# Loading gates, keys and queries four tokens to a packet, with the gate weights issued by ScalarE and the first products on a tile of ones

## The chip, the core and the metric

The kernel runs on one core of a Trainium2 chip. The core has five engines that work side by side and wait for each other by semaphores: TensorE (PE in the profile, with PEld for its weight loads), VectorE (DVE), ScalarE (ACT), GpSimd (POOL) and SyncE (SP, which only issues DMAs here). Sixteen DMA engines move data between the main memory and the core's own memory of 128 partitions. The metric is the device time of one execution in microseconds (us).

## The reference

A gated linear attention over 4 batches, 8 heads, 768 tokens and 48 columns a head, and behind it a mixture of 8 experts that takes each token's 384 columns:

```python
f = 1.0 / (1.0 + np.exp(-f_logit))
for t in range(S):
    state = f[:, :, t, :, None] * state + np.einsum('bhd,bhe->bhde', k[:, :, t], v[:, :, t])
    y[:, :, t] = np.einsum('bhd,bhde->bhe', q[:, :, t], state)
x = y.transpose(0, 2, 1, 3).reshape(B * S, H * D)
logits = x @ w_gate
expert_idx = np.argmax(logits, axis=1)
# each expert takes its first `capacity` tokens, in order
h = np.maximum(np.einsum('ecd,edf->ecf', disp, w1), 0.0)
y = np.einsum('ecf,efd->ecd', h, w2)
# out[i] = gate_w[i] * (the row of y that token i took), 0 for a token that found no place
```

## The kernel before

The tokens are worked on in 24 chunks of 128 (six to a batch). Instead of one token after the other, a chunk uses products of gates: DVE scans the transposed gates once backwards (`Suf`, line 386) and once forwards (`Rq`, line 400), the keys are multiplied by the one and the queries by the other (line 415), and PE then makes the scores of the whole chunk (`psA`, line 426), masks and all, the product with the values (`psY`, line 522), and an update of the state (lines 488 and 508).

The layout of the loads matters here. For gates (`ld_f`), keys and queries (`ld_kq`) a partition holds two tokens that follow each other, for all eight heads: a piece of 2 x 48 numbers is contiguous in the main memory, 384 bytes. A chunk thus takes 64 partitions; gates of two chunks, or the keys and the queries of one, fill the 128. Values (`ld_v`) have one token to a partition, in pieces of 192 bytes. Before the transposes the pieces are written apart into padded tiles: gates by ACT with the sigmoid (`sig`, line 357, into `pf`), keys and queries by a copy (`kq_pad`, line 407 on POOL and later line 409 on ACT, into `kqp`). `transposes` (line 366) then turns 64 partitions at a time, one pair of heads and one of the two tokens in each call, into `psF` (gates) or `psT` (keys and queries) with every second column written.

Chunk by chunk the work runs in slots: slot n has the values of chunk n, the scores of n + 1, keys and queries of n + 2 (`kq_in`) and gates of n + 3 (`f_in`, `decay`). The order in each engine's queue is that in which the code writes it; every engine works through its queue in order. `prologue` writes the work ahead of slot 0: products that have no use but to occupy PE (`keep_busy`, line 376, on the identity matrix that POOL builds), the gates, keys and queries of the first chunks, and the constants that come late (`late_constants`, line 282: four small DMAs that put the gate weights of the experts into `identc`). All loads but one half of the first gates are issued by SP, in one queue. The queue also stops at a load whose buffer is still read. Loads take turns on eight semaphores, so an issue also waits until the one eight places earlier on the same semaphore has landed.

Attention ends at about 144 us; the experts' products follow.

## Time and profile before

| | |
|---|---|
| time, median of 3 runs | 375.02 us (374.31 to 376.33) |
| the profiled execution | 375.17 us |
| its span, first to last instruction | 373.4 us |
| PE busy | 362.1 us, 97% |
| DVE busy | 247.8 us, 66% |
| ACT busy | 223.8 us, 60% |
| POOL busy | 166.5 us, 45% |
| mean granted clock of PE | 0.990 |

Busy time of PE is modelled and pipelined, so 97% does not say that PE works at its peak. The granted clock is a share of 2.4 GHz, so 0.50 is 1.2 GHz. The chain of waits goes back from the last instruction to what released it, step by step. In the timeline, merged instructions stand in one row, and the brackets say how long the engine was idle before it and what ended that.

### The profile page before, as it was taken

Reading aid. Unit: us, or ns where it says so; the run is one execution under the profiler, and the core shown is the slowest. Engines: PE = TensorE matmul, PEld = TensorE weight load, DVE = VectorE, ACT = ScalarE, POOL = GpSimd, SP = SyncE. Lnnn points to the kernel's source line nnn. Section 1 sums busy time; section 2 is a strip of 40 time slices with the busy share of each in tenths; the row PEclk is TensorE's granted clock in tenths of the full one; section 3 lists DMA queues with packets and bytes.
Section 4 is the critical chain, followed back from the end, with each engine's and each line's share of the span. In section 5 each row is a group of like instructions: output and inputs, shape, how many; then the busy total and the mean of one; then the engine's idle time right before and its main releaser. Section 6 shows DMA issues by size and latency. Waiting matters only on the chain.

```text
span 373.4 us, 10082 instructions
## 1 busy us (share of the span) xinstructions
PE 362.1 (97%) x3895; PEld 340.8 (91%) x3895; DVE 247.8 (66%) x533; ACT 223.8 (60%) x458; POOL 166.5 (45%) x275
## 2 busy tenths in 40 slices
PE   8999999999899999999999999999999999999993
PEld 7999898888787889999899999999999999999993
DVE  4898988979687866753676296857757665570300
ACT  3356677877586763255477475759578586583310
POOL 6665556675757675235613702127117244144012
PEclk9999999999899999999999999999999999999997
DMA  8999999999997432476696979799797997721001
GB/s 153 187 177 224 205 207 227 256 214 226 213 227 164 130 114 105 133 237 204 191 239 188 286 196 242 212 187 319 169 204 247 172 208 253 129 94 52 14 23 40
DMA packets 111351, 67.86 MB, mean 182 GB/s; under 512 B 93646, under 2 KB 105844, under 8 KB 111296
## 3 DMA queue, kind: packets, MB, share of 16 engines
q1 hardware_dynamic: 107504, 57.09, 69.1%
q0 software_dynamic: 3520, 9.97, 7.7%
q8 instruction: 32, 0.52, 0.6%
q14 instruction: 23, 0.19, 0.2%
q10 hardware_dynamic: 272, 0.10, 0.1%
HBM read 49.46 MB, written 11.43 MB: 163 GB/s over the span
## 4 chain that ended last, share of the span: by engine, by line
PE 84%; issue 8%; ACT 3%; POOL 2%; DVE 1%; POOLq 1%; ACTq 0%
PE psM L1222 15%; PE psA L754 9%; PE psM L1015 9%; PE psT L754 9%; PE psM L754 7%; PE psA L426 6%; PE psY L522 6%; PE psA L543 5%; PE psT L366 4%; PE psY L468 3%; PE psA L488 3%; PE psT L451 3%; PE psF L366 2%; POOL out_dram L326 2%; PE psA L376 2%
## 5 line engine op out<-in xcount | busy, mean ns | idle before, releaser
L326 POOL DMA_INDIRECT out_dram<-yo,g_ti x30 | 31.3, 1042 | 55.6 <-ACT yo L1019 31.7
L434 POOL TENSOR_SCALAR_AFFINE_SELECT AT<-AT 128x512 f32<-128x512 f32 x48 | 29.4, 637 | 23.3 <-ACT AT L432 23.2
L1015 PE MATMUL psM<-w2h,hh 128*128 128x384 f32 (+2 forms) x112 | 37.5, 340 | 0.0
L1015 PE MATMUL psM<-w2l,hh 128*128 128x384 f32 (+2 forms) x112 | 37.3, 338 | 0.0
L1015 PE MATMUL psM<-w2h,hl 128*128 128x384 f32 (+2 forms) x112 | 37.2, 338 | 0.0
L135 ACT ACTIVATE w2h<-raw 128x768 fp32r<-128x768 f32 x32 | 27.0, 844 | 11.2 <-DMA raw<-in_moe_w_dram 11.2
L1222 PE MATMUL psM<-hh,w2h 128*128 128x440 f32 (+3 forms) x96 | 33.7, 351 | 0.0
L1222 PE MATMUL psM<-hh,w2l 128*128 128x440 f32 (+3 forms) x96 | 33.7, 351 | 0.0
L1222 PE MATMUL psM<-hl,w2h 128*128 128x440 f32 (+3 forms) x96 | 33.6, 350 | 0.0
L144 DVE TENSOR_TENSOR w2l<-raw,w2h 128x768 fp32r<-128x768 f32 x28 | 27.8, 994 | 7.7 <-ACT w2h L135 6.9
L386 DVE TENSOR_TENSOR_SCAN Suf<-psF,direv 112x511 f32<-112x511 f32 x24 | 29.1, 1212 | 4.5 <-PE psF L366 4.5
L432 ACT ACTIVATE AT<-psA 128x512 f32<-128x512 f32 x48 | 26.4, 612 | 8.9 <-PE psA L426 5.6
L1242 POOL COPY yo<-yq 128x384 uint16<-128x384 uint16 (+4 forms) x16 | 11.9, 790 | 40.1 <-DMA yq<-yp 38.2
L426 PE MATMUL psA<-qT,kT 48*128 48x128 f32 x384 | 29.4, 293 | 0.0
L400 DVE TENSOR_TENSOR_SCAN Rq<-psF,d 112x512 f32<-112x512 f32 x24 | 29.4, 1223 | 0.0
L326 POOL DMA_INDIRECT disp<-rows,ri x24 | 24.8, 1034 | 9.5 <-issue 4.3
L144 DVE TENSOR_TENSOR w1l<-raw,w1h 128x1024 fp32r<-128x1024 f32 x21 | 26.5, 1269 | 2.9 <-ACT w1h L135 2.6
L761 DVE SCALAR_TENSOR_TENSOR hl<-psA,hh 128x224 fp32r<-128x224 f32 (+8 forms) x26 | 14.2, 547 | 21.3 <-ACT hh L760 19.3
L559 ACT ACTIVATE rows<-psA 128x384 f32<-128x384 f32 x24 | 11.8, 491 | 26.0 <-PE psA L543 19.6
L522 PE MATMUL psY<-AT,ld_v 128*48 128x128 f32 (+1 forms) x384 | 26.9, 278 | 0.0
L426 PEld LDWEIGHTS psA<-qT,kT 48*128 48x128 f32 x384 | 25.8, 201 | 0.5 <-issue 0.5
L135 ACT ACTIVATE w1h<-raw 128x1024 fp32r<-128x1024 f32 x24 | 24.8, 1060 | 1.9 <-DMA raw<-in_moe_w_dram 1.9
(253 smaller groups left out, 1041.7 us busy)
## 6 DMA issues: line engine op xcount, KB each, us to landing
raw<-in_moe_w_dram SPq DMA_DIRECT2D x24, 512.0 KB
raw<-in_moe_w_dram SPq DMA_DIRECT2D x32, 384.0 KB
ld_kq<-in_k_dram SPq DMA_DIRECT2D x24, 192.0 KB
ld_kq<-in_q_dram SPq DMA_DIRECT2D x24, 192.0 KB
ld_v<-in_v_dram SPq DMA_DIRECT2D x24, 192.0 KB
ld_f<-in_f_logit_dram SPq DMA_DIRECT2D x11, 384.0 KB
xg<-disp SPq DMA_DIRECT2D x6, 589.5 KB
xg<-disp SPq DMA_DIRECT2D x3, 393.0 KB
```

Source lines behind the costliest of these rows:

```text
L135: return nc.scalar.activation(hi, raw, AF.Copy)
L144: engine.tensor_tensor(lo[cs], raw[cs], hi[cs].bitcast(F32), op=ALU.subtract)
L326: ins = nc.gpsimd.indirect_dma_start(out=dst, out_offset=bass.IndirectOffsetOnAxis(ap=idx, axis=0), in_=rows, in_offset=None, bounds_check ...
L386: nc.vector.tensor_tensor_scan(out=_view(Suf[:R], m - 1, [[-1, m]]), data0=_view(F, m, [[-1, m]]), data1=_view(direv[:R], m - 1, [[-1, m]] ...
L400: nc.vector.tensor_tensor_scan(out=Rq[:R], data0=F, data1=d1[:R], initial=0.0, op0=ALU.mult, op1=ALU.max)
L426: nc.tensor.matmul(pas[s][:, p], kTs[n][r, p], qTs[n][r, p], start=True, stop=True)
L432: nc.scalar.activation(AT[:, s], pas[s], AF.Copy)
L434: nc.gpsimd.affine_select(AT[:, s], AT[:, s], pattern=[[0, NP], [1, C]], compare_op=ALU.is_ge, fill=0.0, base=0, channel_multiplier=-1)
L522: nc.tensor.matmul(py[b][64 * g : 64 * g + m, a, :], vt[:, 2 * p + s, :m], AT[:, s, p, :], start=(first(n) and a == 0), stop=(a == NP // 2 ...
L754: nc.tensor.matmul(ph[:, :T], a[:, c, fs], x[:, c, :T], start=(n == 0), stop=(n == 3 * DT - 1))
L1015: nc.tensor.matmul(py[:n], x[:, ks], a[:, ft], start=(ft == 0 and m == 0), stop=(ft == FT - 1 and m == 2))
L1222: nc.tensor.matmul(pys[c][:, :T], a[:, ft, cs], x[:, :T], start=(ft == 0 and n == 0), stop=(ft == FT - 1 and n == 2))
```

## The change

Gates, keys and queries now have four tokens to a partition, in pieces of 4 x 48 numbers (768 bytes). Each partition holds four heads only, so a chunk takes two times 32 partitions: heads 0 to 3 on the first 32, heads 4 to 7 on the next. `load_quads` takes the place of `pairs` and issues a DMA for each half, so that a load of keys, or of queries, is two DMAs, and one of gates for two chunks is four. `transposes` has four tokens and two pairs of heads in its loops instead of two and four; the number of calls is the same, each writes every fourth column of two pairs.

At the start a tile of ones (`hot`, the first 128 columns of the ring of rows, which is now made earlier) is written by DVE, and `keep_busy` multiplies it by itself, eight times first instead of seven. The gates' transposes of chunk 0 get a second stream beside them, on the other 64 partitions, that transposes the ones into a PSUM tile that nobody reads. The sigmoid of chunk 0 is cut in two along the heads. The four DMAs of `late_constants` move from SP to ScalarE's queue, behind the sigmoids of chunk 0. The pad of chunk 0 is cut in keys and queries, and their transposes are made one after the other instead of in turn. The loads of the third keys and queries, of the first values and of the third gates are written later in the code.

```diff
+    ring = abuf.tile([P, RING, W], F32, name="rows", bufs=1)
+    hot = ring[:, 0, :P]
+    nc.vector.memset(hot, 1.0)
...
-                t = apool.tile([P, H, 2, D], F32, name=f"ld_{nm}{i}")
+                t = apool.tile([P, NP, 4, D], F32, name=f"ld_{nm}{i}")
...
-    def pairs(nm, n, nt):
+    def load_quads(t, r, nm, n, queues):
         b, t0 = n // CPB, n % CPB * C
-        return srcs[nm][b, :, t0 : t0 + nt, :].rearrange("h (t j) d -> t h (j d)", j=2)
+        for i, queue in enumerate(queues):
+            queue.dma_start(
+                t[r + 32 * i : r + 32 * i + 32].rearrange("t h j d -> t h (j d)"),
+                srcs[nm][b, NP * i : NP * i + NP, t0 : t0 + C, :].rearrange("h (t j) d -> t h (j d)", j=4),
+            )
...
         if nm == "kq":
             for h, x in enumerate(nm):
-                nc.sync.dma_start(t[64 * h : 64 * h + 64], pairs(x, n, C))
+                load_quads(t, 64 * h, x, n, (nc.sync, nc.sync))
         elif n == 0:
...
+            load_quads(t, 0, nm, 0, (nc.sync, nc.scalar))
         else:
-            nc.sync.dma_start(t, pairs(nm, 2 * n, 2 * C))
+            for h in range(2):
+                load_quads(t, 64 * h, nm, 2 * n + h, (nc.sync, nc.sync))
...
-                nc.sync.dma_start(identc[64 * g : 64 * g + D, b::2, 2 * D :], gates_of[b, g ^ b])
+                nc.scalar.dma_start(identc[64 * g : 64 * g + D, b::2, 2 * D :], gates_of[b, g ^ b])
...
-        cuts = (0, 64, P) if u == 0 else (0, P)
+        cuts = ((0, 64, 0, 2), (0, 64, 2, NP), (64, P, 0, NP)) if u == 0 else ((0, P, 0, NP),)
...
+            if (r1, h1) == (64, NP):
+                late_constants()
...
-        for p in range(NP):
-            for j in range(2):
+        for p in range(2):
+            for j in range(4):
                 for t, src, h in dsts:
                     r = slice(64 * h, 64 * h + 64)
                     nc.tensor.transpose(
-                        t[:R, p, j::2], src[r, j, 2 * p : 2 * p + 2].rearrange("t s d -> t (s d)")[:, :R], ident[r, r]
+                        t[:R, p::2, j::4], src[r, j, 2 * p : 2 * p + 2].rearrange("t s d -> t (s d)")[:, :R], ident[r, r]
                     )
+                if beside is not None:
+                    nc.tensor.transpose(beside[:R, p::2, j::4], hot[64:, :R], ident[64:, 64:])
...
-            nc.tensor.matmul(pw, ident, ident, start=True, stop=True)
+            nc.tensor.matmul(pw, hot, hot, start=True, stop=True)
...
+        beside = None if ns[0] else psA.tile([P, NP, C], F32, name="psA")
...
+        made = [(psT.tile([P, NP, C], F32, name="psT"), kqp[n % 2], h) for h in range(2)]
+        pts = transposes(*made) if n else [transposes(one)[0] for one in made]
...
-        keep_busy(7)
+        keep_busy(8)
         nc.scalar.activation(warm, direv[:, :1], AF.Sigmoid)
         sig(0)
+        load("kq", 2)
+        load("v", 0)
+        load("f", 2)
         f_in(0)
...
-        late_constants()
```

The first rows of ACT's queue before; `ld_f` are gates as loaded, `pf` after the sigmoid, `identc` holds the gate weights, `AT` are scores:

```order
L214 DMA ld_f_100<-in_f_logit_dram 64x4x96
L772 ACT_TABLE_LOAD
L772 ACTIVATE warm<-direv 128x1
L357 ACTIVATE pf_118<-ld_f_100 64x16x48 x2
L357 ACTIVATE pf_120<-ld_f_101 128x16x48
L432 ACTIVATE AT<-psA 128x512 x2
```

The same rows now:

```order
L201 DMA ld_f_102<-in_f_logit_dram 32x4x192
L784 ACT_TABLE_LOAD
L784 ACTIVATE warm<-direv 128x1 [waits DVE_49]
L362 ACTIVATE pf_120<-ld_f_102 64x4x2x48 [waits DMAHW1_49,DMAHW0_49]
L362 ACTIVATE pf_120<-ld_f_102 64x4x2x48
L287 DMA identc<-in_moe_w_gate_dram 48x2x8 [waits Pool_49]
L287 DMA identc<-in_moe_w_gate_dram 48x2x8
L287 DMA identc<-in_moe_w_gate_dram 48x2x8 [waits DMAHW3_49]
L287 DMA identc<-in_moe_w_gate_dram 48x2x8 [waits DMAHW5_49]
L362 ACTIVATE pf_120<-ld_f_102 64x16x48 [waits DMAHW6_49,DMAHW0_49]
```

The first sigmoid is in two parts, and the four DMAs now stand between the gates of chunk 0 and those of chunk 1; two of them wait for a load that used their semaphore before.

SP's queue before, from its start, with the waits (`DMAHW` is a semaphore of loads):

```order
L214 DMA ld_f_100<-in_f_logit_dram 64x4x96
L210 DMA ld_kq_103<-in_k_dram 64x8x96
L210 DMA ld_kq_103<-in_q_dram 64x8x96
L224 DMA ld_f_100<-in_f_logit_dram 64x8x96
L210 DMA ld_kq_104<-in_k_dram 64x8x96
L210 DMA ld_kq_104<-in_q_dram 64x8x96
L216 DMA ld_f_101<-in_f_logit_dram 128x8x96
L210 DMA ld_kq_105<-in_k_dram 64x8x96 [waits DMAHW0_49]
```

The same stretch now:

```order
L201 DMA ld_f_102<-in_f_logit_dram 32x4x192
L201 DMA ld_kq_105<-in_k_dram 32x4x192 x2
L201 DMA ld_kq_105<-in_q_dram 32x4x192 x2
L201 DMA ld_f_102<-in_f_logit_dram 32x4x192
L201 DMA ld_f_102<-in_f_logit_dram 32x4x192 [waits DMAHW0_49]
L201 DMA ld_kq_106<-in_k_dram 32x4x192 [waits DMAHW2_49]
L201 DMA ld_kq_106<-in_k_dram 32x4x192 [waits DMAHW4_49]
L201 DMA ld_kq_106<-in_q_dram 32x4x192 [waits DMAHW6_49]
L201 DMA ld_kq_106<-in_q_dram 32x4x192 [waits DMAHW7_49]
L201 DMA ld_f_103<-in_f_logit_dram 32x4x192 [waits DMAHW0_49]
```

The sequence of tensors is the same; each stands there in two or four pieces, and the first wait for a semaphore comes two tensors earlier. Behind the prologue all engines have their instructions in the order that they had.

## Rows read from the trace of the kernel before

**Rows 1.** The page, busy us, share of the span and instructions of each engine

```profile
PE 362.1 (97%) x3895; PEld 340.8 (91%) x3895; DVE 247.8 (66%) x533; ACT 223.8 (60%) x458; POOL 166.5 (45%) x275
```

**Rows 2.** Chain of waits, 0 to 60 us: start, us on the chain, what

```profile
1.83 3.35 PE psA L376 x14
...
5.21 1.07 PE psF L366 x8
...
8.28 1.03 PE psT L366 x16
...
12.36 1.81 PE psA L426 x16
...
49.35 0.95 PE psA L426 x15
50.30 0.45 PE psT L366 x16
```

**Rows 3.** Windows: length, busy us (instructions) by engine, granted clock, DMA share, GB/s

```profile
5.00:10.00 5.00, 4.98 (x41) 4.44 (x40) 3.31 (x6) 0.90 (x2) 1.74 (x5) 1.00 1.28 214
...
100.00:102.00 2.00, 2.00 (x32) 2.00 (x30) 1.25 (x2) 0.00 (x0) 0.90 (x3) 0.50 1.09 231
```

**Rows 4.** Chain of waits of the whole span, products with the values around 100 us

```profile
89.10 0.88 PE psY L522 x16
...
94.76 0.88 PE psY L522 x16
...
102.04 1.57 PE psY L522 x16
```

**Rows 5.** Timeline 0 to 20 us, DVE, and PE's keys: start, us, work [idle before]

```profile
0.99 0.48 DVE L227 MEMSET direv<- 128x512 f32 x1 [0.99 <-PEq L1476]
...
6.31 1.22 DVE L386 TENSOR_TENSOR_SCAN Suf<-psF,direv 112x511 f32<-112x511 f32 x1 [3.83 <-PE psF L366]
...
9.35 0.69 DVE L415 TENSOR_TENSOR kT<-psT,Suf 112x512 f32<-112x512 f32 x1 [0.34 <-PE psT L366]
...
15.05 1.22 DVE L386 TENSOR_TENSOR_SCAN Suf<-psF,direv 112x511 f32<-112x511 f32 x1 [0.64 <-PE psF L366]
...
18.41 0.69 DVE L415 TENSOR_TENSOR kT<-psT,Suf 112x512 f32<-112x512 f32 x1 [0.67 <-PE psT L366]
...
19.02 0.68 DVE L415 TENSOR_TENSOR qT<-psT,Rq 112x512 f32<-112x512 f32 x1
...
19.84 0.33 PEld L451 LDWEIGHTS psT<-ident,kT 64*128 64x128 f32 x8 [0.17 <-DVE qT L415]
```

**Rows 6.** Timeline, ACT, POOL and SP at the loads of the prologue and of chunks 6, 7

```profile
4.22 0.84 ACT L357 ACTIVATE pf<-ld_f 64x768 f32<-64x768 f32 x1 [1.15 <-DMA ld_f<-in_f_logit_dram]
...
7.12 0.82 POOL L407 COPY kqp<-ld_kq 128x768 f32<-128x768 f32 x1 [1.12 <-DMA ld_kq<-in_q_dram]
...
7.92 0.84 ACT L357 ACTIVATE pf<-ld_f 64x768 f32<-64x768 f32 x1 [2.87 <-DMA ld_f<-in_f_logit_dram]
...
14.54 3.40 SPq L282 DMA_DIRECT2D identc<-in_moe_w_gate_dram  x4
...
28.25 0.84 ACT L357 ACTIVATE pf<-ld_f 128x768 f32<-128x768 f32 x1 [0.32 <-DMA ld_f<-in_f_logit_dram]
```

**Rows 7.** Timeline of SP's queue: start, us of issuing, what

```profile
2.52 0.64 SPq L210 DMA_DIRECT2D ld_kq<-in_q_dram  x1
...
5.23 0.63 SPq L216 DMA_DIRECT2D ld_f<-in_f_logit_dram  x1
...
156.12 1.48 SPq L122 DMA_DIRECT2D raw<-in_moe_w_dram  x3
```

**Rows 8.** Waits of 20 to 125 us: us in total, times, longest

```profile
POOL kqp L407 <- DMA ld_kq<-in_q_dram: 5.5, 2, 4.2
...
ACT pf L357 <- DMA ld_f<-in_f_logit_dram: 0.3, 1, 0.3
```

More of the change, by code (lines that the diff above doesn't have):

```diff
@@ L190 @@
         for i in range(n):
[L191 removed]
+            t = apool.tile([P, 4, NP, 64], F32, name=f"{nm}{i}")
             nc.gpsimd.memset(t[:, :, :, D:], 0.0)
             made.append(t)
[L195 removed]
+    def load_quads(t, r, nm, n, queues):
         b, t0 = n // CPB, n % CPB * C
[L197 removed]
+        for i, queue in enumerate(queues):
[3 more added lines that the diff above has]
+            )
     def load(nm, n):
@@ L354, in sig, with transposes @@
             return
-        cuts = (0, 64, P) if u == 0 else (0, P)
-        for r0, r1 in zip(cuts, cuts[1:]):
+        cuts = ((0, 64, 0, 2), (0, 64, 2, NP), (64, P, 0, NP)) if u == 0 else ((0, P, 0, NP),)
+        for r0, r1, h0, h1 in cuts:
             pace["ins"] = nc.scalar.activation(
-                pf[u % 2][r0:r1, :, :, :D], loaded("f", u)[r0:r1].rearrange("t h j d -> t j h d"), AF.Sigmoid
+                pf[u % 2][r0:r1, :, h0:h1, :D],
+                loaded("f", u)[r0:r1, h0:h1].rearrange("t h j d -> t j h d"),
+                AF.Sigmoid,
             ).ins
-    def transposes(*dsts):
-        for p in range(NP):
-            for j in range(2):
+            if (r1, h1) == (64, NP):
+                late_constants()
+    def transposes(*dsts, beside=None):
+        for p in range(2):
+            for j in range(4):
                 for t, src, h in dsts:
@@ L375, in keep_busy @@
         for _ in range(m):
-            nc.tensor.matmul(pw, ident, ident, start=True, stop=True)
+            nc.tensor.matmul(pw, hot, hot, start=True, stop=True)
     def f_in(*ns):
         made = [(psF.tile([P, NP, C], F32, name="psF"), pf[n // 2 % 2], n % 2) for n in ns]
-        for n, F in zip(ns, transposes(*made)):
+        beside = None if ns[0] else psA.tile([P, NP, C], F32, name="psA")
+        for n, F in zip(ns, transposes(*made, beside=beside)):
             Fs[n] = F
@@ L406, in kq_pad @@
             if n - 3 < PAD_ACT:
-                nc.gpsimd.tensor_copy(kqp[n % 2][:, :, :, :D], src)
+                for r in (slice(0, 64), slice(64, P)) if n == 0 else (slice(0, P),):
+                    nc.gpsimd.tensor_copy(kqp[n % 2][r, :, :, :D], src[r])
             else:
@@ L411, in kq_in @@
     def kq_in(n):
-        pts = transposes(*((psT.tile([P, NP, C], F32, name="psT"), kqp[n % 2], h) for h in range(2)))
+        made = [(psT.tile([P, NP, C], F32, name="psT"), kqp[n % 2], h) for h in range(2)]
+        pts = transposes(*made) if n else [transposes(one)[0] for one in made]
         for nm, pt, by, made in (("kT", pts[0], Sufb[n % 2], kTs), ("qT", pts[1], Rqs.pop(n), qTs)):
@@ L545, in rows_pe @@
         return px
-    ring = abuf.tile([P, RING, W], F32, name="rows", bufs=1)
     def row_at(n):
```

9 lines of the change are left out of this document (2 added, 7 removed).

## The prediction

> **What bounds the kernel now.** I read the page first: PE is busy for 97% of the span [rows 1]. That is a sum over stages, so I read the chain of waits for the first 60 us [rows 2]. It holds PE and almost nothing else from 1.83 us on: fillers, transposes of gates, of keys and queries, scores. To the end of attention PE's instructions stand back to back, so what the change can move is the point at which that dense stream begins; the weights' stage is untouched.
>
> The reader should compare equal groups in [rows 2]. Sixteen score products take 1.81 us at 12.36 and fifteen take 0.95 us at 49.35; sixteen paired transposes take 1.03 us at 8.28 and 0.45 us at 50.30. The same work costs twice as much early: this is the 1.2 GHz level. The granted-clock column shows 1.00 there and 0.50 only around 100 us [rows 3], so for the start I believe the durations and not the column: PE is slow from its first product until about 18 us, although it stands hardly still.
>
> DVE is the second reading [rows 5]. Its first scan starts at 6.31 us, when the transposed gates of chunk 0 are there, and the queries of chunk 2 end at 19.02 + 0.68 = 19.70 us. In these 13.39 us it waits 0.34 + 0.64 + 0.67 = 1.65 us, each time for transposes by PE; the rest, 11.74 us, is its own work. Right behind it, at 19.84, PE's transposes of keys wait for DVE and no more for PE's own queue: there the prologue hands over to the dense stream. So the prologue is bounded by DVE's chain: its start (6.31), its work (11.74), its waits for a slow PE (1.65).
>
> DMA comes third. After 20 us ACT waited 0.3 us for gates and POOL 5.5 us for queries [rows 8], and PE did not stop for either. Transfers matter only where DVE or PE is reached: the gates of chunks 0 and 1 at 4.22 and 7.92 us, the first queries at 7.12 [rows 6].
>
> **The change part by part.** The sum is made against the profiled execution: 375.17 us, 373.4 of it span, 0.15 above the median of the three runs (375.02).
>
> *Fillers on a tile of ones.* PE waits until 1.83 for the identity that POOL builds. DVE's first memset starts at 0.99 [rows 5] and 512 columns take 0.48 us, so 128 columns take 0.12 to 0.2 and PE can start at about 1.2, 0.6 us earlier. Fourteen instructions take 3.35 us [rows 2], 0.24 each; two more cost 0.4 to 0.5. At an unchanged clock the gates' transposes then start 0.1 to 0.2 earlier than 5.21: I take 0.15. The first sigmoid is in two parts; 768 columns take 0.84 us from 4.22 [rows 6], so half is there at about 4.65 and does not hold PE.
>
> *The clock.* Fillers now run without a break from 1.2 us into transposes that are doubled by a second stream on the other 64 rows, then into four more fillers: PE stays filled over all rows until about 8 us, where it was half filled in the gates' transposes. I expect the high level somewhere between 4.5 and 8 us instead of at 18. Eight single transposes take 1.07 us now, sixteen paired ones 0.45 us at the high level [rows 2]; if the rise falls into them half of the 0.6 us is won. I take 0.3. DVE's first scan then starts at 6.31 - 0.15 - 0.3 = 5.86.
>
> *DVE's waits.* With transposes and scores at half their time, PE is ready before DVE at 15.05 and 18.41; I leave 0.3 of the 1.65 us. The queries of chunk 2 end at 5.86 + 11.74 + 0.3 = 17.9 instead of 19.70. The gain is 1.8 us, and as PE is dense behind it, it passes to the end whole. Lower end: only the 0.15, and less than nothing in the next point.
>
> *Keys before queries in chunk 0.* They alternated over the two halves of the rows (16 in 1.03 us); now eight and eight run one after the other, each as long as the gates' eight (1.07 slow, about half of it fast). That adds 1.0 us to PE ahead of the gates of chunk 1 if the clock is low, 0.5 if high. The cover: DVE is in its two scans until 2.70 us after its start (6.31 to 9.35 less 0.34 of waiting), so at the high level nothing shows. At the low level it shows with about 0.4 us, since DVE took the gates of chunk 1 at once when its queries were done.
>
> *Gate weights on ScalarE.* Four issues took 3.40 us on SP [rows 6]. On ACT they stand behind the two half sigmoids, from about 5.0 to 8.4, and the third sigmoid is queued behind them; it began at 7.92 when its gates landed. It would end at 9.2, its transposes at about 9.7. DVE needs them at 5.86 + 2.70 + 1.3 = 9.86. The cover is 0.1 to 0.2 us; I put it at nothing, with 0.5 us in the range. Two of the four also wait for transfers issued before them (the order's rows), which I place before 7 us.
>
> *Loads of four tokens.* Descriptors of 768 bytes instead of 384, half as many, but twice (keys, queries) to four times (gates) as many issues on SP, and SP's queue is in order. Up to the gates of chunks 6 and 7 SP now makes 42 issues, formerly 24 with the four for the gate weights. An issue now stands 0.68 us behind the last (2.52 to 5.23 is four of them), three issues of one row per partition take 1.48 us, 0.49 each [rows 7]. With 0.49 SP is through them at 0.8 + 42 x 0.49 = 21.4 us, with 0.68 at 29.4; ACT used them at 28.25 [rows 6]. I take 0.5, as the new pieces have 128 descriptors like those rows, and then nothing is lost; nothing is won either, since PE never stood for a load.
>
> The Trainium skill, "DMA: Bandwidth & Descriptors", Specifications, puts the least transfer for full rate at 512 bytes, which speaks for the new packets. By that alone I would credit shorter loads; by [rows 8] the sum takes none of it, because no wait for a load reached PE.
>
> Edits with one answer: the ring tile made earlier, the split pad of chunk 0 on POOL (0.82 us in two halves), three loads written later in the code with the same place in SP's order: nothing.
>
> Sum: 375.17 - 1.8 = 373.4 us, which is 0.43% below the median of 375.02.
>
> **The rivals.**
>
> *The clock stays low.* Fillers of this kind ran from 1.83 to 5.2 and again for 2 us at 6.2, and the level stayed low; the new run is longer by one product and fuller by the second stream, not of another kind. Then the start wins 0.15, the unpaired keys and queries cost 0.4, and the third sigmoid 0.1: about 375.5 us. The Trainium skill, "TensorE: Matmul & The Clock Gate", Part 4, says that transposes don't count as busy for the gate the way products do; by it the doubled transposes would not help, and this rival is what is left. The trace bears it out halfway: the transposes and scores after 14 us did bring the rise.
>
> *The clock rises and falls again.* After the rise PE has little to do while DVE scans; around 100 us the level fell after a stretch with waits [rows 3]. Then only the start (0.45) and the first wait (0.34) are won: 375.17 - 0.8 = 374.4.
>
> *SP falls behind (the slower side).* If an issue keeps its 0.68 us, or the queue waits for each transfer eight places earlier, the gates for chunks 6 and 7 are issued at 29.4 and land some 2.5 to 3 us later, at 32: ACT stands about 4 us where it now goes on at 28.25, with the evictions of the next chunk behind it. Beyond that, two chunks need 14 issues, 9.5 us, as long as two slots (94.76 - 89.10 = 5.66 is a long one [rows 4]). One part of the wait is hidden by PE's work in hand: 375.17 - 1.0 + 3.4 = 377.6. It decides from about 0.62 us per issue on. The Trainium skill, the same page on DMA, Rules for kernel authors, advises one transfer over 128 partitions rather than two over halves, since halves share the engines. By it the split buys nothing and only this price is left; no row here shows it yet.
>
> *The fall at 100 us goes too.* Values follow values there after 102.04 - 94.76 = 7.28 us instead of 5.66, and take 1.57 instead of 0.88 [rows 4]: 2.3 us. Another start may shift it away: 373.4 - 2.3 = 371.1. It may as well bring a second one, so this gets little.
>
> **How the numbers follow.** Forecast (373.4, 372.7 to 374.2 by itself) 0.50; low clock (375.5) 0.18; rise and fall (374.4) 0.13; no fall at 100 (371.1) 0.11; SP behind (377.6) 0.08. A measurement of this kernel can tell about 0.5%, 1.9 us, from no change: faster means below 373.1, slower above 376.9. Faster: the 0.11, and under half of the forecast's share, its lower edge, 0.23, together 0.34. Slower: SP behind, and the upper edge of the low clock, 0.10. Within: 0.56. The range leaves out the SP rival and most of the 371.1: 371.7 to 375.9.
>
> **What would show it.** In the trace after: fillers from about 1.2 us; sixteen scores in about 1 us, not 1.8, at 10 to 12 us; DVE's first scan before 6.0 and PE's first transposes of keys into psT at about 18; ACT with no wait for gates around 26 us; SP's issues 0.5 us apart. I am wrong if scores stay at 1.8 us in the prologue, if ACT or POOL wait for loads by more than 2 us between 15 and 35 us, or if paired transposes, which now write every fourth column, take more than 0.46 us for sixteen at the high level.

## The result, and the profile after

The changed kernel takes 377.31 us (median of 22 runs, 374.81 to 380.76), the kernel before beside it 375.01 us: a ratio of 1.0053, with a 95% interval of 1.0031 to 1.0074. Forecast were 373.4 us and a range up to 375.9. It is slower, by 2.3 us, and 3.9 us above the forecast. The profiled execution took 377.05 us (span 375.3). In two later sets of runs the same kernel stood at 1.0075 (1.0042 to 1.0108) and 1.0041 (1.0015 to 1.0066): the sign is safe, its size by the three ratios is 0.4 to 0.75 per cent.

The prologue came out almost as forecast. The timeline of PE in the kernel after (start, us, engine and line, work, idle time before and what ended it):

```profile
1.13 3.57 PE L387 MATMUL psA<-rows 128*128 128x128 f32 x16 [1.13 <-DVE rows L177]
...
10.62 1.11 PE L440 MATMUL psA<-qT,kT 48*128 48x128 f32 x16
...
15.56 0.66 PE L375 MATMUL psT<-ident,kqp 64*112 64x64 f32 x16 [0.91 <-POOL kqp L420]
...
17.74 0.46 PE L465 MATMUL psT<-ident,kT 64*128 64x64 f32 x8
```

and that of DVE:

```profile
5.47 1.22 DVE L398 TENSOR_TENSOR_SCAN Suf<-psF,direv 112x511 f32<-112x511 f32 x1 [2.85 <-PE psA L379]
...
16.87 0.68 DVE L429 TENSOR_TENSOR qT<-psT,Rq 112x512 f32<-112x512 f32 x1
```

Sixteen scores take 1.11 us, not the 1.81 of [rows 2] (a chain's measure; 2.02 on the timeline's), so the high level is there at 10.6 us. DVE's first scan starts 0.84 us earlier than in [rows 5], the queries of chunk 2 end at 17.55 instead of 19.70, and PE's first keys come at 17.74 (forecast "about 18", before 19.84). What is new is the third line: PE stands 0.91 us for POOL, and POOL for a load.

Waits of the kernel after, 20 to 125 us (us in total, times, longest), which answer to [rows 8]:

```profile
POOL kqp L420 <- DMA ld_kq<-in_q_dram: 13.9, 6, 3.9
...
PE psA L502 <- DMA ld_v<-in_v_dram: 2.0, 1, 2.0
ACT pf L362 <- DMA ld_f<-in_f_logit_dram: 1.4, 1, 1.4
```

POOL waits for queries 13.9 us instead of 5.5, and now PE itself waits for a load, which it does nowhere in the profile of before up to 125 us. Two of POOL's copies, from its timeline:

```profile
23.72 0.83 POOL L420 COPY kqp<-ld_kq 128x768 f32<-128x768 f32 x1 [3.42 <-DMA ld_kq<-in_q_dram]
...
33.34 0.82 POOL L420 COPY kqp<-ld_kq 128x768 f32<-128x768 f32 x1 [3.87 <-DMA ld_kq<-in_q_dram]
```

The table follows the start of the products with the values (L522 before, L536 after) from slot to slot, in us, for the profiles that the text uses. The names are explained with the experiments.

| kernel | slot 0 | slot 1 | slot 3 | slot 9 | slot 15 | slot 23 |
|---|---|---|---|---|---|---|
| before | 18.76 | 23.82 | 33.98 | 63.06 | 94.52 | 142.91 |
| before, again (e8) | 17.56 | 22.73 | 33.46 | 63.19 | 93.23 | 138.46 |
| after | 16.70 | 22.70 | 33.35 | 66.64 | 98.16 | 144.10 |
| after, again (e12) | 16.20 | 22.88 | 34.39 | 64.06 | 96.54 | 142.29 |
| after, again (g4) | 17.37 | 23.39 | 33.73 | 63.05 | 95.37 | 144.53 |
| new start alone (e1) | 16.46 | 22.79 | 34.88 | 63.57 | 94.68 | 143.42 |
| after, loads as before (g3) | 16.79 | 23.21 | 34.02 | 63.30 | 95.62 | 141.44 |
| before, loads cut (e3) | 19.27 | 26.39 | 42.29 | 75.10 | 109.97 | 156.59 |
| before, less load (h2) | 17.29 | 22.46 | 32.53 | 61.70 | 93.46 | 139.16 |
| g3, less load (h1) | 17.09 | 22.61 | 32.68 | 62.72 | 94.12 | 139.76 |
| after, less load (h3) | 17.49 | 23.94 | 34.01 | 63.67 | 95.16 | 140.86 |

In the first profile of after the lead of 2.06 us at slot 0 is 1.12 at slot 1 and 0.63 at slot 3; by slot 9 it has become a lag of 3.58 us. That second step is in the chain of waits of after from 40 to 52 us (start, us, what):

```profile
40.76 0.43 SPq L201
...
41.23 0.43 SPq L201
...
41.77 5.50 DMA ld_v<-in_v_dram
47.27 0.14 issue
47.40 0.64 PE psA L502 x13
```

SP issues load behind load without a pause, the values of chunk 6 are issued at 41.77 and land 5.50 us later, and PE, which had been ready, has stood. Behind that stall the granted clock falls. Windows of the kernel after (length, busy us (instructions) of PE, PEld, DVE, ACT, POOL, then granted clock, DMA share, GB/s):

```profile
5.00:10.00 5.00, 3.85 (x49) 3.26 (x44) 4.37 (x7) 0.84 (x1) 3.70 (x9) 1.00 0.69 165
10.00:15.00 5.00, 3.81 (x72) 3.43 (x72) 4.93 (x10) 2.77 (x6) 2.99 (x33) 1.00 0.75 185
...
45.00:48.00 3.00, 0.98 (x31) 0.81 (x28) 1.89 (x6) 2.36 (x5) 0.07 (x1) 1.00 0.92 241
48.00:52.00 4.00, 4.00 (x51) 3.62 (x52) 3.40 (x9) 0.79 (x3) 2.46 (x4) 0.59 0.93 193
```

In 45 to 48 us PE is busy for 0.98 us of three, and in the next four the mean granted clock is 0.59, most of them at the lower of the two levels. Not every execution has this: e12 and g4, the same kernel, are at slot 9 at 64.06 and 63.05 us. So the four microseconds of slots 6 to 8 are one execution's; what all three share is that the lead at slot 0 (1.4 to 2.6 us on the first profile of before) is gone by slot 9.

Last, SP's queue in the kernel after (start, us of issuing, what):

```profile
11.73 3.01 SPq L201 DMA_DIRECT2D ld_f<-in_f_logit_dram  x4
...
15.80 0.85 SPq L201 DMA_DIRECT2D ld_kq<-in_q_dram  x2
...
22.91 2.75 SPq L201 DMA_DIRECT2D ld_f<-in_f_logit_dram  x4
...
26.23 3.09 SPq L201 DMA_DIRECT2D ld_f<-in_f_logit_dram  x4
...
30.32 0.90 SPq L201 DMA_DIRECT2D ld_kq<-in_q_dram  x2
```

Two issues that wait for nothing take 0.85 us, 0.43 each, less than the 0.5 of the forecast. But four loads of gates take 2.75 to 3.09 us. From 9.36 to 36.09 us SP makes 43 issues, 0.62 us each on average. In the program's order every load from the ninth on first waits on one of eight semaphores, which go round: on the landing of the transfer eight places earlier. Two consecutive pieces of gates and two of keys, as the order of after has them:

```
L201 DMA ld_f_104<-in_f_logit_dram 32x4x192 [waits DMAHW3_49]
L201 DMA ld_f_104<-in_f_logit_dram 32x4x192 [waits DMAHW4_49]
L201 DMA ld_kq_105<-in_k_dram 32x4x192 [waits DMAHW5_49,Pool_49]
L201 DMA ld_kq_105<-in_k_dram 32x4x192 [waits DMAHW6_49]
```

How much of the 0.62 us is such a wait stands in the waits of SP itself, 9 to 36 us:

```profile
SPq L201 <- DMA ld_v<-in_v_dram: 1.1, 1, 1.1
```

That is one wait for a landing, 1.1 us of 27. The rest is issuing: 43 times 0.43 us and some 0.05 us to the next issue are about 20.5 us, and a few single issues took up to 1.6 us, for a reason that the profile does not show. So SP's queue is full by the number of its issues, and hardly by landings. The queries that POOL gets at 33.34 us were issued from 30.32 us on, behind eight pieces of gates (those of 22.91 and 26.23).

### The profile page after: what moved, and what is told of

It is laid out like the page before. It is cut to its first block, busy times and chain, and to the rows that moved or that the text cites. A ratio compares the mean times of both kernels' runs of the same rounds, so it can differ in the third digit from the quotient of the medians.

```text
span 375.3 us, 10238 instructions
## 1 busy us (share of the span) xinstructions
PE 359.2 (96%) x3905; PEld 337.0 (90%) x3905; DVE 246.7 (66%) x534; ACT 224.3 (60%) x459; POOL 167.7 (45%) x276
## 4 chain that ended last, share of the span: by engine, by line
PE 72%; issue 10%; DMA 7%; POOL 4%; ACT 3%; SPq 2%; DVE 1%; POOLq 1%; ACTq 0%
PE psM L1236 15%; PE psA L766 9%; PE psT L766 9%; PE psM L1029 8%; PE psM L766 6%; PE psY L536 5%; PE psA L557 5%; PE psA L440 3%; PE psT L375 3%; PE psT L465 3%; PE psY L482 2%; PE psA L502 2%; SPq L201 2%; POOL out_dram L331 2%; DMA ld_f<-in_f_logit_dram 2%
## 5 line engine op out<-in xcount | busy, mean ns | idle before, releaser
L144 DVE TENSOR_TENSOR w2l<-raw,w2h 128x768 fp32r<-128x768 f32 x28 | 26.9, 959 | 4.5 <-ACT w2h L135 3.7
L1256 POOL COPY yo<-yq 128x384 uint16<-128x384 uint16 (+4 forms) x16 | 11.1, 736 | 41.3 <-DMA yq<-yp 39.8
L144 DVE TENSOR_TENSOR w1l<-raw,w1h 128x1024 fp32r<-128x1024 f32 x21 | 25.6, 1227 | 4.4 <-ACT w1h L135 4.3
L440 PE MATMUL psA<-qT,kT 48*128 48x128 f32 x384 | 27.8, 282 | 0.0
L536 PE MATMUL psY<-AT,ld_v 128*48 128x128 f32 (+1 forms) x384 | 26.9, 279 | 0.0
L440 PEld LDWEIGHTS psA<-qT,kT 48*128 48x128 f32 x384 | 24.4, 191 | 0.5 <-issue 0.5
```

The source lines that it names most:

```text
L144: engine.tensor_tensor(lo[cs], raw[cs], hi[cs].bitcast(F32), op=ALU.subtract)
L440: nc.tensor.matmul(pas[s][:, p], kTs[n][r, p], qTs[n][r, p], start=True, stop=True)
L536: nc.tensor.matmul(py[b][64 * g : 64 * g + m, a, :], vt[:, 2 * p + s, :m], AT[:, s, p, :], start=(first(n) and a == 0), stop=(a == NP // 2 ...
```

## The experiments

The theory to begin with (A): a load lands some 5 us after its issue whether it is large or small, only eight may be on the way, and the change makes 14 transfers out of 7 for every two chunks, of half or a quarter the size. Rivals: the smaller destinations of 32 rows are slow in themselves (B), the gates' pieces alone do it (F), or the loads are not it and the start or the gate weights on ScalarE are (D). Kernels of one set ran on one chip beside the kernel before; sets need not share a chip, so each ratio is to the kernel before of its own set (374.16, 373.77, 374.62, 375.17 and 374.18 us in sets 1 to 5).

### Set 1: which part costs

**e6**, the changed kernel with the loads and layouts of before:

```diff
-                load_quads(t, 64 * h, x, n, (nc.sync, nc.sync))
+                nc.sync.dma_start(t[64 * h : 64 * h + 64]..., pairs(x, n, C))
-            for h in range(2):
-                load_quads(t, 64 * h, nm, 2 * n + h, (nc.sync, nc.sync))
+            nc.sync.dma_start(t..., pairs(nm, 2 * n, 2 * C))
```

> The changed kernel with the loads and layouts of before (two tokens to a packet, one transfer for 64 or 128 partitions); the tile of ones, the doubled transposes, the gate weights on ScalarE and the unpaired keys and queries of chunk 0 stay. Theory A (the loads of four tokens are late because SP may have only eight transfers on the way, and each is now half or a quarter as large): the 2 us won at the start stay, 373.0 us (372.3 to 374.2), POOL waits under 6 us for loads as before, PE does not wait for values of chunk 6, and the clock does not fall at 48.7 us. Theory D (the loads are not it; the earlier start or the gate weights on ScalarE make the stage fall behind): 376.5 to 378, with POOL waiting 10 us or more between 12 and 60 us.

Measured: 373.15 us, ratio 0.9963 (0.9929 to 0.9997): inside the range of theory A and against D. The same kernel comes back as g3 in set 4, where it is not faster than before.

**e2**, the kernel before with only the new loads (with the transposes that their layout needs, and the three loads that the change writes later written later here too):

```diff
-                nc.sync.dma_start(t[64 * h : 64 * h + 64], pairs(x, n, C))
+                load_quads(t, 64 * h, x, n, (nc.sync, nc.sync))
-            nc.sync.dma_start(t, pairs(nm, 2 * n, 2 * C))
+            for h in range(2):
+                load_quads(t, 64 * h, nm, 2 * n + h, (nc.sync, nc.sync))
```

> The kernel before with only the loads of four tokens and their layout; fillers on the identity, gate weights on SP, keys and queries paired. Theory A: transfers set the pace of the first nine slots, so the later start costs little on top: 377 to 379.5 us, the values' products of slot 9 at 66.5 to 68 us (before 63.06, after 66.64), POOL waits for loads 9 us or more. Theory D: as before, 374.5 to 375.6 us, the loads hidden.

Measured: 377.02 us, ratio 1.0093 (1.0058 to 1.0127). The new loads alone make the kernel slower. The slots were earlier than expected (slot 9 at 63.91), and the profile held a surprise. Its PE begins, on fillers of the identity:

```profile
5.07 0.66 PE L370 MATMUL psF<-ident,pf 64*112 64x64 f32 x8
```

Eight transposes in 0.66 us where [rows 2] has 1.07: the level was up at 5 us without a tile of ones and without a second stream.

**e3**, the kernel before with each load cut in two by heads, gates in four. Bytes, packets of 384 bytes and the 64 rows stay:

```diff
-                nc.sync.dma_start(t[64 * h : 64 * h + 64], pairs(x, n, C))
+                for hs in (slice(0, 4), slice(4, H)):
+                    nc.sync.dma_start(t[64 * h : 64 * h + 64, hs], pairs(x, n, C)[:, hs])
-            nc.sync.dma_start(t, pairs(nm, 2 * n, 2 * C))
+            for g in range(2):
+                for hs in (slice(0, 4), slice(4, H)):
+                    nc.sync.dma_start(t[64 * g : 64 * g + 64, hs], pairs(nm, 2 * n + g, C)[:, hs])
```

> The kernel before with each load of gates, keys and queries cut in two transfers by heads (gates in four), the packets of 384 bytes, the 64 rows and the order unchanged. Theory A (transfers on the way): as many transfers as the changed kernel, each as small, so the same holes in the DMA row and 377 to 380 us, SP's issues each waiting for the transfer eight places earlier. Theory B (the pieces are slow because they go to 32 partitions, or because of 768-byte packets): as before, 374.5 to 375.7 us, 20 to 50 us at some 209 GB/s.

Measured: 392.31 us, ratio 1.0479 (1.0432 to 1.0527), far beyond what theory A had asked for, and flatly against B. Cutting the loads in two, with nothing else changed, costs 18 us, part of it in stretches at the low level: over 20 to 50 us the mean granted clock is 0.88, in the kernel before 1.00.

The reason is not the one that theory A gives. SP's queue in e3:

```profile
14.54 2.58 SPq L219 DMA_DIRECT2D ld_f<-in_f_logit_dram  x4
17.24 1.26 SPq L211 DMA_DIRECT2D ld_kq<-in_k_dram  x2
18.54 1.27 SPq L211 DMA_DIRECT2D ld_kq<-in_q_dram  x2
19.86 0.60 SPq L205 DMA_DIRECT2D ld_v<-in_v_dram  x1
```

Nine issues follow each other in 5.92 us, 0.66 us apart, of which 0.61 is the issue, and in 9 to 36 us SP's waits show none for a landing. The places on the way are free, and SP is occupied with issuing alone. The gates of chunks 6 and 7, which SP issued at 21.46 us in the kernel before, go out from 29.35 us on, and ACT stands 5.12 us for them. So the count of transfers decides, as theory A has it, but through the time of one issue in a single queue.

DMA in 20 to 50 us (packets, bytes, mean rate, packets by size), of e3:

```profile
DMA packets 14236, 4.47 MB, mean 149 GB/s; under 512 B 13973, under 2 KB 14229, under 8 KB 14229
```

of the kernel before:

```profile
DMA packets 18216, 6.28 MB, mean 209 GB/s; under 512 B 17697, under 2 KB 18209, under 8 KB 18209
```

and of the kernel after:

```profile
DMA packets 12314, 5.75 MB, mean 192 GB/s; under 512 B 7014, under 2 KB 12307, under 8 KB 12307
```

e3 and after issue as many loads of as many bytes; they differ in the packets, 384 bytes against 768. So the change does two things that work against each other: twice the transfers takes the rate from 209 to 149 GB/s, and the larger packets bring it back to 192. At least part of that step is again SP's: one of its issues takes 0.61 us in e3 and 0.43 us in after, and in 20 to 50 us the DMA engines are busy for a share of only 0.67 in e3 (1.10 in before, 0.86 in after). The Trainium skill, "DMA: Bandwidth & Descriptors", Specifications, puts the least transfer for full rate at 512 bytes; the step from 149 to 192 GB/s goes the way of that rule, but does not test it.

**e5**, the changed kernel with the gates alone as before, 11 transfers for two chunks:

```diff
-            for h in range(2):
-                load_quads(t, 64 * h, nm, 2 * n + h, (nc.sync, nc.sync))
+            nc.sync.dma_start(t..., pairs(nm, 2 * n, 2 * C))
```

> The changed kernel with the gates alone loaded as before (two tokens to a packet, one transfer of 128 rows), keys and queries still four tokens in halves: 11 transfers for two slots, where the changed kernel has 14 and before 7. Theory A: about half of the loss goes, 374.0 to 375.5 us. Theory B (32 partitions): keys and queries are two thirds of the pieces, 375.5 to 376.8 us. Theory D: 376.5 to 378.

Measured: 371.41 us, ratio 0.9921 (0.9883 to 0.9959), better than any theory had it. Its page has the time from issue to landing beside the size (DMA issues: count, KB each, median us to landing):

```profile
ld_kq<-in_k_dram SPq DMA_DIRECT2D x48, 96.0 KB, 5.4
ld_kq<-in_q_dram SPq DMA_DIRECT2D x48, 96.0 KB, 4.5
ld_v<-in_v_dram SPq DMA_DIRECT2D x24, 192.0 KB, 5.7
ld_f<-in_f_logit_dram SPq DMA_DIRECT2D x11, 384.0 KB, 5.6
```

Here a quarter of the bytes lands 0.2 to 1.1 us sooner. In e9 below, which has the same loads, the difference is larger:

```profile
ld_kq<-in_q_dram SPq DMA_DIRECT2D x48, 96.0 KB, 4.2
...
ld_f<-in_f_logit_dram SPq DMA_DIRECT2D x11, 384.0 KB, 7.0
```

So a load does not land after some 5 us whatever its size, as theory A has it, though four times the bytes take less than twice as long. With 5 us a transfer and eight on the way, one could start every 0.6 us, close to the mean of SP's queue in after; by the waits of SP in after and in e3 that agreement is chance.

### Set 2: the start by itself

**e1**, the kernel before with only the tile of ones, sixteen fillers and the second stream:

```diff
+    hot = ring[:, 0, :P]
+    nc.vector.memset(hot, 1.0)
-            nc.tensor.matmul(pw, ident, ident, start=True, stop=True)
+            nc.tensor.matmul(pw, hot, hot, start=True, stop=True)
+                if beside is not None:
+                    nc.tensor.transpose(beside[:R, p, j::2], hot[64:, :R], ident[64:, 64:])
-        keep_busy(7)
+        keep_busy(8)
```

> The kernel before with the new start alone: eight and more fillers on a tile of ones, the gates' first transposes doubled by a second stream; loads, layouts, gate weights on SP and paired keys and queries as before. If the tile of ones and the doubled transposes bring the early rise of the clock and the prologue passes to the end: 372.5 to 373.5 us, scores at 10 to 12 us in 1.1 us and not 2.0. If the rise comes as early without them (the kernel with only the new loads rose at 5 us on identity fillers): 373.8 to 375.3, no difference from the kernel before on the same chip.

Measured: 374.11 us, ratio 1.0026 (0.9990 to 1.0062): nothing won, though slot 0 starts 2.3 us earlier than in the first profile of before. By slot 3 it is 0.9 us late. Waits of e1, 20 to 125 us:

```profile
POOL kqp L413 <- DMA ld_kq<-in_q_dram: 11.9, 5, 4.5
```

With the loads exactly as before, POOL now waits 11.9 us for queries instead of 5.5. The lead at the start went into the loads; a second loss of this profile, near 124 us, is shown under set 4.

**e8**, the kernel before itself, looked at again.

> The kernel before, unchanged, looked at again: when does TensorE's level rise, and where does it fall? If the rise is fixed by what PE does, sixteen scores at 12 us take 2.0 us as in the first profile, values of slot 0 start at 18.8 and the fall comes at 100 us. If it varies between executions, the scores take 1.1 us, values start at 16 to 17, and the fall is elsewhere or missing.

Measured: 371.65 us in that one run. The same kernel, another history: the scores are still slow, but the level rises right behind them, at about 14 us and not 18, and there is no fall at 100 us. PE of e8:

```profile
12.44 1.92 PE L426 MATMUL psA<-qT,kT 48*128 48x128 f32 x16
14.19 0.50 PE L366 MATMUL psF<-ident,pf 64*112 64x64 f32 x6
```

So 1.2 of the 2.06 us by which after leads at slot 0 belong to the execution that I had in front of me, not to the kernel.

**e9**, the kernel before with only keys and queries four tokens to a packet (the same three loads written later as in e2):

```diff
-                nc.sync.dma_start(t[64 * h : 64 * h + 64], pairs(x, n, C))
+                load_quads(t, 64 * h, x, n, (nc.sync, nc.sync))
```

> The kernel before with only keys and queries loaded four tokens to a packet in halves; gates in pairs, fillers, gate weights and order as before: 11 transfers for two slots. Theory A (transfers on the way): the larger packets free the DMA engines and 11 transfers still fit, so as fast as the version with the new start or up to 1.5 us slower: 371.5 to 373.5 us. Theory of the start (the 2 to 3 us of that version are the start's): 374 to 375.5 us.

Measured: 371.73 us, ratio 0.9961 (0.9918 to 1.0005). As theory A had it: the new packets for keys and queries, without the new start, are inside the range expected of them, and what the start adds to them (e5, in another set) can't be told from nothing, the intervals overlap.

**e7**, the changed kernel with values loaded by GpSimd:

```diff
-            nc.sync.dma_start(t[:, :, :D], srcs[nm][b, :, t0 : t0 + C, :]...)
+            nc.gpsimd.dma_start(t[:, :, :D], srcs[nm][b, :, t0 : t0 + C, :]...)
```

> The changed kernel with the loads of values issued by GpSimd instead of SP, everything else as changed. These loads then take no place in SP's rotation of eight: 12 of 14 transfers are left in it. Theory A: SP's other loads come earlier, by 1 us for two slots, PE does not wait for values, 373 to 375.5 us. Theory A2 (each transfer costs the DMA engines time, whichever queue it comes from): 376.5 to 378 us, with the DMA row as full of holes as in the changed kernel. POOL pays for each issue, which it can here since it waits for loads.

Measured: 375.54 us, ratio 1.0021 (0.9972 to 1.0069). The loads did what theory A says: 207 GB/s in 20 to 50 us instead of 192, and of 20 to 125 us

```profile
POOL kqp L420 <- DMA ld_kq<-in_q_dram: 2.8, 2, 1.8
```

2.8 us of waiting for queries instead of 13.9. The time is at the upper edge of theory A's range, and the profiled execution ran at the low level from about 9 us for over 13 us. It shows that loads taken out of SP's queue shorten the waits. Whether by the places on the way or by SP's time for an issue it does not tell apart, nor what the waits are worth in time.

### Sets 3 and 4: number of transfers, the gates, or the chip

**e10**, the changed kernel with keys and queries as before and gates in four pieces, 10 transfers; **e11**, e5 with the two transfers that zero rows moved from slots 1 and 3 to 4 and 5; **e12**, the changed kernel again.

```diff
(e10)
-                load_quads(t, 64 * h, x, n, (nc.sync, nc.sync))
+                nc.sync.dma_start(t[64 * h : 64 * h + 64]..., pairs(x, n, C))
(e11, on e5)
-        if n in (1, 3):
-            zero_disp(0 if n == 1 else NE)
+        if n in (4, 5):
+            zero_disp(0 if n == 4 else NE)
```

> The changed kernel with keys and queries loaded as before (two tokens, one transfer for 64 rows); gates four tokens in four transfers of 32 rows: 10 transfers for two slots. Theory A (the count of transfers decides, whichever tensor they belong to): at 4.1 to 5.6 us from issue to landing, eight places carry one transfer in 0.5 to 0.7 us, 10 take 5 to 7 us of the 9.4 us that two slots last, so no loss: 371.5 to 374 us, POOL's waits 6 to 12 us, none of PE for values. Theory F (the gates' four small pieces are harmful in themselves, keys and queries are not): 376 to 378 us as the changed kernel.

> The version with gates in pairs and keys and queries four tokens to a packet, with the two transfers that zero the first expert's and the spare rows (393 KB each) issued in slots 4 and 5 instead of 1 and 3. If the early slots wait for loads (POOL waited 11 us for queries, the longest 4.6 us at 34 us, right behind these two transfers), they come out of the way of keys and queries of chunks 7 and 8: 369.5 to 371.5 us, that wait under 2 us. If PE has caught up by slot 9 in any case: 371 to 372, as without the move.

> The changed kernel, unchanged, timed on the same chip as the other two and looked at again. Theory A: POOL waits 10 us or more for keys and queries again and the values of slot 9 start past 65.5 us (66.64 in the first profile), 376 to 378 us. If the loss of the first profile was its one fall of the clock at 48.7 us: slot 9 at 63.5 to 64.5 and 373 to 375 us.

Measured: e10 377.20 us, 1.0084 (1.0051 to 1.0116); e11 375.70 us, 1.0040 (1.0007 to 1.0074); e12 377.21 us, 1.0075 (1.0042 to 1.0108). e10 spoke for F and against the count. e12 had the time of theory A but not its signs: slot 9 came at 64.06 us, and POOL waited 7.6 us for queries. e11 was a miss for both: the longest wait of POOL fell from 4.6 to 2.4 us, and the kernel was not faster. Since e5 and e10 had not run on the same chip, the four combinations of loads were then put side by side: **g1** = e5, **g2** = e10, **g3** = e6, **g4** = after.

> The changed kernel with the gates alone loaded as before, again, now on one chip with the next three. Theory A (number of transfers, 11): between the kernel with 7 and the one with 14. Theory F (the gates' four pieces): as fast as the kernel with all loads as before or up to 2 us faster, ratio to before 0.990 to 0.997. Theory chip: ratio within 0.4% of the other three.

> The changed kernel with keys and queries loaded as before and the gates four tokens in four pieces, again: 10 transfers. Theory A: not slower than the kernel with 11, ratio to before 0.992 to 1.000. Theory F: as the changed kernel, 1.005 to 1.010. Theory chip: within 0.4% of the others.

> The changed kernel with all loads as before (7 transfers), again. Theories A and F: ratio to before 0.993 to 1.001. Theory chip: within 0.4% of the others.

> The changed kernel itself (14 transfers) beside the three. Theories A and F: ratio to before 1.004 to 1.010, at least 0.5% over the kernel with the gates as before. Theory chip: within 0.4% of the other three.

Measured, by the number of transfers for two chunks:

| kernel | transfers | us | ratio to before (95%) |
|---|---|---|---|
| g3, all loads as before | 7 | 375.68 | 1.0019 (0.9993 to 1.0044) |
| g2, gates in four pieces | 10 | 376.12 | 1.0012 (0.9988 to 1.0036) |
| g1, keys and queries four tokens | 11 | 376.13 | 1.0019 (0.9997 to 1.0042) |
| g4, the changed kernel | 14 | 376.99 | 1.0041 (1.0015 to 1.0066) |

In this set F falls: g2 is not slower than g1. But e10, the same kernel as g2, was as slow as the changed kernel in its own set. The chip, or the set, turns out to matter as much as the edit: one and the same kernel, e5 and g1, stands at 0.9921 (0.9883 to 0.9959) and at 1.0019 (0.9997 to 1.0042). What holds inside this set is weak: medians rise with the number of transfers, by 1.3 us from 7 to 14 (the intervals of the two overlap), and only the changed kernel is safely slower than before. Among 7, 10 and 11 nothing can be told.

g3 also shows where the start's gain goes when the loads are as before. Its chain of waits from 12 to 24 us:

```profile
13.08 6.77 DMA ld_kq<-in_q_dram
...
20.00 0.83 POOL kqp L426
...
20.87 0.66 PE psT L381 x16
```

The queries of a chunk are on the chain for 6.77 us, then POOL's copy, then PE's transposes. And the early level does not stay. PE of g3, then its window:

```profile
11.53 2.02 PE L446 MATMUL psA<-qT,kT 48*128 48x128 f32 x16
```

```profile
11.00:14.00 3.00, 3.00 (x38) 3.00 (x37) 2.53 (x5) 1.26 (x2) 2.54 (x31) 0.50 1.37 187
```

Up before 5 us, granted 0.50 from 11 to 14 us, behind a stretch in which PE waited four times for POOL and ACT: the scores are as slow as in the kernel before.

One more place decides between these profiles, and it lies behind the early loads. From slot 20 to slot 23 most profiles take 18.6 to 20.8 us, but e7 and g4 take 22.3, e1 24.1 and e2 24.4. There PE waits until the tokens of the first expert have been read back (`xg`, from `disp`), and behind the wait the level falls. PE of e1, of e2 and of g4, then a window of g4:

```profile
125.52 0.69 PE L722 MATMUL psF<-ident,xg 128*128 128x128 f32 x2 [2.73 <-DMA xg<-disp]
```

```profile
125.78 0.69 PE L725 MATMUL psF<-ident,xg 128*128 128x128 f32 x2 [3.32 <-DMA xg<-disp]
```

```profile
127.72 0.44 PE L730 MATMUL psF<-ident,xg 128*128 128x128 f32 x2 [2.08 <-DMA xg<-disp]
```

```profile
128.00:132.00 4.00, 4.00 (x51) 3.59 (x50) 1.66 (x7) 0.96 (x3) 2.07 (x3) 0.57 0.31 115
```

In e3, e5, e6, e8 and e9 the same wait is 0.7 to 1.8 us and the level stays; the other profiles have none. At slot 20 g4 (122.19 us) is level with g3 (122.25), and e2 (119.02) with e8 (118.75, another set), so the 2.7 and 3.6 us by which these two executions are longer arose here. It is not shown to come from the new loads: e1 has it with the loads as before, after and e12 are without it.

### Set 5: the loads out of the way

**h1** (on g3), **h2** (on before), **h3** (on after):

```diff
             for h, x in enumerate(nm):
+                if x == "q" and 3 <= n <= 5:
+                    continue
```

> The changed kernel with loads as before (gates, keys and queries in pairs), and the queries of chunks 3, 4 and 5 not loaded (those of chunks 0, 1 and 2 stand in for them): 590 KB and three transfers less in the first 25 us; the rest is computed as ever. Theory L (loads set the pace of slots 1 to 3): the start's gain passes, values of slot 3 at 31.9 to 32.5 us where they stood at 34.0, and 1.5 to 2 us less than the kernel before with the same left out: 373.0 to 373.8 us. Theory S (the gain is lost in the clock or elsewhere): values of slot 3 at 33.5 to 34, 375 us, level with the kernel before.

> The kernel before with the queries of chunks 3, 4 and 5 not loaded (those of chunks 0 to 2 stand in). Theory L: its loads just keep up, so nothing changes: values of slot 3 at 33.6 to 34.0 us, ratio to before 0.997 to 1.001. Theory S: the same.

> The changed kernel with the queries of chunks 3, 4 and 5 not loaded (those of chunks 0 to 2 stand in), so six of the small transfers less. Theory L: its loss is one of loads too, values of slot 3 at 32 to 32.6 us and 373.3 to 374.8 us, below the kernel before. Theory S: 376 to 377.5 us.

Measured: h1 373.19 us, 0.9986 (0.9949 to 1.0023); h2 372.73 us, 0.9959 (0.9921 to 0.9998); h3 373.91 us, 0.9992 (0.9958 to 1.0027). Slot 3 comes at 32.68 in h1 (g3 34.02) and at 32.53 in h2 (before 33.98, e8 33.46). So the loads do set the pace of slots 1 to 3, in the kernel before as well: theory L is right there, and its claim that before "just keeps up" is wrong. But the start still gives nothing, h1 is no faster than h2. The windows say why. h1, then h2:

```profile
11.00:14.00 3.00, 3.00 (x36) 3.00 (x37) 2.71 (x6) 0.96 (x2) 2.48 (x31) 0.52 1.39 186
```

```profile
11.00:14.00 3.00, 3.00 (x36) 2.78 (x36) 2.96 (x6) 0.84 (x1) 2.54 (x31) 1.00 1.37 186
```

In h1 the level fell at the scores, as in g3. In h2, on identity fillers, it rose at about 14 us as in e8 (the 1.00 of its window is again the column that [rows 3] showed to be no guide at the start), and both arrive at slot 0 at 17.1 and 17.3 us. The changed kernel comes down to the time of the kernel before when these loads are gone (0.9992, with them 1.0041 to 1.0075), so its loss is largely one of loads; but h3 stays 1.2 us above h2, the two intervals overlap, and its slot 3 (34.01) did not move as expected.

## Why the prediction was wrong, point by point

**Right.** Fillers from 1.13 us (said: 1.2), the level up before 8 us, DVE's first scan at 5.47 (said: 5.86), queries of chunk 2 at 17.55 (17.9), PE's keys at 17.74 (18), one issue 0.43 us (0.5), paired transposes that write every fourth column at their old 0.66 us on the timeline. Gate weights on ScalarE cost nothing that shows: the third sigmoid began at 7.17 us, before 7.92.

**Wrong: "as PE is dense behind it, it passes to the end whole."** Forecast were -1.8 us. Measured, with the loads as before, were +0.5 us in g3 (375.68 to 375.17, an interval that includes zero), +0.3 in e1, and -1.0 in e6, the same kernel as g3 in another set (0.1 to 2.7 us faster by its interval, so that set alone does not exclude the forecast). PE is not dense behind the start, and the traces show three places where the lead went. The loads bound slots 1 to 3 as well: without the queries of three chunks slot 3 comes 1.34 us earlier in h1 than in g3, with the same history of the clock, and 0.93 to 1.45 us earlier in h2 than in the two profiles of before. It was there to be read: POOL waited 5.5 us for queries in [rows 8], and the DMA share in [rows 3] was 1.28 at 5 to 10 us. I took "PE did not stop for a load" for slack; it only said that the load was not the later of two. The level is not won for good: in g3 and h1 it fell again at 11 us, my rival "rises and falls again", which I had priced at 0.13 and with 0.8 us still won. And near 124 us PE waits for the first expert's tokens, in e1 for 2.73 us, with the level down behind it.

**Wrong: the base of the sum.** It subtracted from one profiled execution. In that one the level rose at 18 us; in e8 and h2, with the same instructions on PE, at about 14, in e3 at 10, in e2 and e9, on the same fillers, at 5. Of the 2.15 us by which the queries of chunk 2 came earlier a large part was no property of the kernel: they end at 18.71 us in e8 and at 18.09 in g4, 0.6 us apart.

**Wrong: "nothing is lost" by loads of four tokens.** This term was put at nothing, and it measured 0.9% in e2 (3.5 us by the ratio, 2.9 by the medians), which is the kernel before with these loads alone. In set 4 it is smaller and not clear of noise: 1.3 us by the medians of g4 and g3. The way of reckoning, issues times the time of one, was right: the step that failed is "I take 0.5 [...] and then nothing is lost". SP was to be through its 42 issues at 21.4 us and was through at 25.66, 0.59 us each, and over 9.36 to 36.09 us the mean was 0.62, just the point from which I had said the rival decides. An issue that waits for nothing was even cheaper than forecast (0.43); the step from one issue to the next and the few long issues were missing. The other half of that rival, "or the queue waits for each transfer eight places earlier", counted for little: 1.1 us in 27 in after, none in e3. The rival's landing time was too short as well, 2.5 to 3 us against 4.2 to 5.7 for the pieces and the values in e5 and e9. I gave it 0.08.

**Half right: the rival's price.** SP falling behind was put at 377.6 us, and 377.31 was measured. The agreement is partly chance: its 2.4 us hold a gain of 1.0 us at the start that was not there, and ACT, which was to stand about 4 us for the gates of chunks 6 and 7, stood 1.4 us; the longer waits were POOL's, for queries.

**Open.** Why the same kernels stand 0.6 to 1.0% apart from set to set, and so whether gates in one piece with keys and queries in four (e5, 0.9921; g1, 1.0019) are worth having. How much of the changed kernel's loss is the waits themselves and how much the falls of the level behind them, which differ between executions. Why single issues of SP take up to 1.6 us. No version here is shown to beat the kernel before in every set.

## What to carry to other kernels

Before a change cuts loads into more pieces, count the transfers per stage and queue, take from the trace how far apart the issues stand when the queue never rests, and compare the product with the stage. Look also whether the queue waits for landings; here it hardly did. Larger packets did not pay here for twice the number of transfers. An engine that never stands for a load has slack only if the engine that hands it the data has some too; follow the wait one step further back before passing a gain on to the end. And where the clock's level changes inside a profile, look at a second execution before counting what it costs as something a change can win.

## What the runs showed of the hardware that was not expected

Four times the bytes landed less than twice as late: 4.5 and 5.4 us for 96 KB and 5.6 for 384 KB in e5, 4.2 and 5.3 against 7.0 in e9. One issue of SP took 0.61 us for a piece in 384-byte packets (e3) and 0.43 us for one as large in 768-byte packets (after). Twice the transfers at the same packets took the rate from 209 to 149 GB/s (e3), with SP issuing without a pause.

The rise of TensorE's level at the start varied between 5 and 18 us over kernels that all begin with fourteen products on the identity (e2 and e9 5, e3 10, e8 and h2 14, before 18). With the tile of ones it was up between 4 and 7 us in all fourteen profiles, and fell again inside the first 26 us in eight of them; on the identity it fell there in two of six (e3, e9).

ScalarE's waits for the keys' transposes differ by set, whatever the kernel. Waits of the kernel before, 60 to 125 us:

```profile
ACT kn L457 <- PE psT L451: 2.7, 5, 0.6
```

The same row, of 2.4 us or more, stands in the profiles of after and of sets 3 to 5, and of sets 1 and 2 only in e3's (2.1 us), where all is late; e8, the same kernel, has no such wait, and its slots 16 to 20 take 20.36 us instead of 22.16, part of which is before's fall at 100 us. What causes it was not found.
